# Attention before two MLPs on one core: score transposes as two 64-row halves, chained between value products and scores

## The chip, the cores and the metric

One core of a Trainium2 chip runs the whole program in one launch. The metric is the device time in microseconds (us) of that core, taken as the median of several runs. The engines are TensorE (PE; its weight loads are listed as PEld), VectorE (DVE), ScalarE (ACT), GpSimd (POOL) and the DMA queues, some of which SyncE (SP) issues.

## The reference

Attention with a causal mask and a forgetting bias, for 4 batches of 8 heads, 576 positions and 64 features per head, and then two MLPs over 2304 tokens of width 512 (hidden width 2048):

```python
scores = scale * np.matmul(q, k.transpose(0, 1, 3, 2))
cum = np.cumsum(np.maximum(s, 0.0), axis=-1)
bias = -(cum[:, :, :, None] - cum[:, :, None, :])
scores = np.where(causal, -1000000000.0, scores + np.minimum(bias, 0.0))
attn = np.exp(scores - max); attn = attn / (sum + 1e-09)
x = (attn @ v) as 2304 x 512
h = relu(x @ w_in) ** 2;  x = h @ w_out          # first MLP
h = leaky_relu(x @ w2_in, 0.01);  out = h @ w2_out   # second MLP
```

All weights of the MLPs come as 64-bit floats and are turned into 32-bit words on the chip.

## The kernel before, in words

**Attention** (`attention`, line 650) works through 16 pairs of heads. A pair takes seven steps (`STEPS`, line 77): a kind and a head `e`. Kind 0 is the first two row tiles of 128 queries, kinds 2 and 3 the third and the fourth, kind 4 the last 64 rows of both heads at once. One step is one *slot* `y` of the loop at line 775; there are 7 x 16 = 112 slots (`end`) and some more to drain. In what follows a pair's slots are counted from its own start (`k0`), so that slot 7 of a pair is slot 0 of the next.

For each kind the score products (`scores`, line 445; matmuls at lines 468 and 456) fill one PSUM bank for each head. For kinds 0, 2 and 3 each head has its own 64 rows of the array (`64*128` in the profile); kind 4 uses all 128 rows. `maxima` (line 473, DVE) masks and reduces, `exponentials` (line 504, ACT) writes the tile `t`. Two slots later (`LAG = 2`) `flip` (line 512) transposes `t` on TensorE in 128x128 pieces (line 518, and line 532 for the last 64 keys) into a PSUM bank with the tag `tr`, one head at a time, and lines 784 and 786 copy it to `pT` with DVE or ACT. `values` (line 537, matmuls at line 554) multiplies by v: the first 256 queries (region 0) in slot 5, the other 320 (region 1) in slot 9. Both heads share a bank, each with 64 columns of the array (`128*64`). `gather` (ACT, line 564) takes the result out one slot later, `inverse` and `widen` prepare the reciprocal row sums, `spread` (lines 584 and 587) transposes them, `scale` (lines 593 to 598) multiplies, and `store` (line 729) writes the pair's result to the DRAM tile `xscr` in slot 12.

**Work beside attention.** The first MLP's up product (`up1`, line 618, matmuls at line 642) goes over 5 blocks of tokens (`BLOCKS`); blocks 0 to 2 are filled in between the attention slots by `fill` (line 746), in three parts a slot. Block j may begin behind slot `START[j] = 28 * (j + 1) + 10`; blocks 0 and 1 are spread so that they end 5 slots before the next start (line 756). Their input is read from `xscr` and rounded into two parts (`up1_x`, line 606: an SP DMA in its first step, ACT line 602 and DVE line 603 in its second) at the slots `START[j]` plus the pairs of gaps in line 713, one pair for each of the four chunks of 128 features. Weight chunks are turned into words by `load_w` (slots 11 to 54) and by `convert` (19 chunks, line 740, from slot `end - 49` on). `later` holds these jobs by slot.

**The order on an engine.** The program's order is a proposal: a scheduler with a simulated timeline reorders instructions within their dependences. `in_order` (line 316) chains the instructions of an engine from a given place on; `after` (line 308) keeps what is issued inside it behind given instructions. PSUM has 4 banks for `tr`, 2 for `h`, and 2 that are one buffer `S` for scores. From pair 5 on (`x >= PLAIN`, `AHEAD = 20` score groups) one group of scores is held ahead, before that two, and the products of the first five pairs are in plain fp32 and not in split parts.

```python
tiles = ((0, 0, P), (1, P, 3 * P)) if kind == 0 else ((kind, 0, (kind + 1) * P),)
...
jobs = flip(at, zx, *STEPS[zs], live.pop(z))
for i, (out, src) in enumerate(jobs):
    if STEPS[zs][1] == 0 and (i == 0 or zx > PLAIN):
        nc.vector.tensor_copy(out, src)
    else:
        nc.scalar.activation(out, src, AF.Copy)
```

After attention come blocks 3 and 4, the first MLP's down product and the second MLP (`down`, `up`, line 839), which the change does not touch.

Of the kernel before, what the change touches and what calls it, by code (L numbers as in the profile page):

```python
# [23 lines left out]
def attention_then_two_mlps(  # L24
# [24 lines left out]
    nc = tc.nc  # L49
# [16 lines left out]
    EARLY = (1, 7, 6, 5)  # L66
    LEAD = 3
    BEFORE = 19
    TB, VB, YB = 3, 4, 2
    GB1, XS, XF = 3, 5, 3  # L70
    QK_SCALE = 1.0 / float(D) ** 0.5
    PASSES = ((0, 0), (0, 1), (1, 0))
# [26 lines left out]
    def bank(tag):  # L99
        return ps.tile([P, 512], F32, tag=tag, name=tag, bufs=dict(tr=4, h=2)[tag])  # L100
# [236 lines left out]
    def running_sums(at, ag):  # L337

        sp, cum = [at.tile([BH, S], F32, tag="t", name="t", bufs=TB) for _ in range(2)]
        one, neg = [at.tile([BH, S], F32, tag="pT0", name="one", bufs=2) for _ in range(2)]  # L340
        ka = at.tile([BH, 2, S], F32R, tag="pT1", name="ka", bufs=2)
        nc.sync.dma_start(sp, s.rearrange("b h t -> (b h) t"))
        nc.gpsimd.memset(one, 1.0)
        nc.gpsimd.memset(neg, -1.0)
        nc.vector.memset(f32(ag[:, 1]), 0.0)
        for e in range(2):
            nc.gpsimd.memset(f32(ag[64 * e:64 * e + 4, 1]), -1.0)
        nc.vector.memset(f32(ag[:, 0]), 1.0)
        yield
        nc.vector.tensor_scalar(sp, sp, 0.0, 1.0 / QK_SCALE, ALU.max, ALU.mult)  # L350
        raw["sums"] = nc.vector.tensor_tensor_scan(cum, one, sp, 0.0, ALU.mult, ALU.add).ins
        nc.vector.tensor_copy(ka[:, 0], cum)
        nc.vector.tensor_tensor(ka[:, 1], cum, f32(ka[:, 0]), ALU.subtract)
        h0, h1 = pairs[0].h
        for z in range(2):
            raw["sent"] = nc.sync.dma_start(f32(ag[z:z + 65:64, 1]), f32(ka[h0:h1 + 1:h1 - h0, z])).ins
            nc.scalar.dma_start(f32(ag[2 + z:z + 67:64, 0]), f32(ka[h0:h1 + 1:h1 - h0, z]))
        yield
        nc.gpsimd.dma_start(aug[:, 0:2, 1], f32(ka))
        stored = nc.gpsimd.dma_start(aug[:, 2:4, 0], f32(ka))  # L360
        with after(stored.ins):
            nc.gpsimd.dma_start(aug[:, 0:2, 0], one.unsqueeze(1).to_broadcast([BH, 2, S]))
            nc.gpsimd.dma_start(aug[:, 2:4, 1], neg.unsqueeze(1).to_broadcast([BH, 2, S]))
# [145 lines left out]
                                        accum_out=sums[:, s0:s0 + 1])  # L509
        return done.ins  # L510

    def flip(at, x, kind, e, t):

        p = pairs[x]
        w = 3 * P if kind == 0 else min((kind + 1) * P, 4 * P)
        tr = bank("tr")
        for c in range(w // P):
            nc.tensor.transpose(tr[:, c * P:(c + 1) * P], t[:, c * P:(c + 1) * P], ident)  # L518
        trv = tr[:, :w].rearrange("p (c i) -> p c i", i=P)
        if kind == 0:  # L520
            p.pT[0, e] = at.tile([P, 3 * P], F32, tag="pT0", name="pT0", bufs=2)
            return [(p.pT[0, e], tr[:, :w])]
        if kind < 4:
            if kind == 2:
                p.pT[1, e] = at.tile([P, 4, NR1], F32, tag="pT1", name="pT1", bufs=2)
            off = kind * P - R
            return [(p.pT[1, e][:, 0:kind + 1, off:off + P], trv)]
        jobs = []
        for h in range(2):
            jobs.append((p.pT[1, h][:, :, 2 * P:], trv[:, :, 64 - 64 * h:P - 64 * h]))  # L530
        tr = bank("tr")
        nc.tensor.transpose(tr[:, :P], t[:, S - P:], ident)
        p.pX = at.tile([P, 2, 64], F32, tag="pX", name="pX")
        jobs.append((p.pX.rearrange("p h i -> p (h i)"), tr[:, :P]))
        return jobs

    def values(x, region):

        p = pairs[x]
        po = bank("tr")  # L540
        n = R if region == 0 else NR1
        mm = []
        for c in range(2 if region == 0 else 5):
            if region == 0:
                mm.append((c, c * P, [p.pT[0, e][:, c * R:R + c * P] for e in range(2)]))
            elif c < 4:
                a = max(0, c * P - R)
                mm.append((c, a, [p.pT[1, e][:, c, a:] for e in range(2)]))
# [101 lines left out]
    def attention(at, mg, mx):  # L650
# [59 lines left out]
        for j in range(B):  # L710
            for c in range(KC):
                job = up1_x(mx, j, c, XS)
                for gap in ((-8, -6), (-7, -4), (-5, -3), (-5, -2))[c]:
                    at_slot(START[j] + gap, step, job)

        for x in range(len(pairs)):
# [23 lines left out]
        for ch in range(BEFORE):  # L740
            job = convert(*divmod(ch, FC), stage, nc.sync, 3)
            for gap in range(6):
                at_slot(end - 5 * BEFORE // 2 - 2 + 5 * ch // 2 + gap, step, job)
        units, block, done = None, -1, 0

        def fill(y, part):

            nonlocal units, block, done
            anchor = pairs[-1].anchor if y >= end + 3 else None
            if units is None and block + 2 < B and y > START[block + 1]:  # L750
                block, done = block + 1, 0
                units = up1(mg, block)
            if units is None:
                return
            a = START[block]
            stop = START[block + 1] - 5 if block + 2 < B else end + 10

            def parts(z, part):
                return (z - a) * 3 + part

            while units is not None and done * parts(stop, -2) < parts(y, part + 1) * (4 * FC + 1):
                if block == B - 2 and anchor is not None:
                    with tc.issue_after(anchor):
                        step_units()
                else:
                    step_units()
# [5 lines left out]
            done += 1  # L772

        live, anchors = {}, [None, None]
        for y in range(end + 13):
            x, st = divmod(y, n)
            z = y - LAG
            jobs = []
            if 0 <= z < end:
                zx, zs = divmod(z, n)  # L780
                jobs = flip(at, zx, *STEPS[zs], live.pop(z))
                for i, (out, src) in enumerate(jobs):
                    if STEPS[zs][1] == 0 and (i == 0 or zx > PLAIN):
                        nc.vector.tensor_copy(out, src)  # L784
                    else:
                        nc.scalar.activation(out, src, AF.Copy)
            if y < end:
                args = maxima(at, x, *STEPS[st])
                live[y] = args[0]
                behind = [args[-1], exponentials(*args[:-1])]  # L790
            fill(y, 0)
            if y + 1 < end and STEPS[(y + 1) % n][1] == 0:
                last = len(KINDS) * x + KINDS.index(STEPS[st][0])
                while asked <= last + (2 if last + 2 < AHEAD else 1):
                    scores(asked // len(KINDS), KINDS[asked % len(KINDS)])
                    asked += 1
            for px in (x - 1, x):
                if not 0 <= px < len(pairs):
                    continue
                k0 = y - n * px  # L800
                if k0 == 6:
                    gather(at, px, 0, pairs[px].po)
                if k0 == 8:
                    scale(px, 0, pairs[px].rb)
                if k0 == 10:
                    gather(at, px, 1, pairs[px].po)
                if k0 == 12:
                    scale(px, 1, pairs[px].rb)
                    store(px)
                if k0 == 5:  # L810
                    pairs[px].po = values(px, 0)
                if k0 == 9:
                    pairs[px].po = values(px, 1)
# [6 lines left out]
                if k0 == 7:  # L820
                    pairs[px].rb = spread(px, 0)
                if k0 == 11:
                    pairs[px].rb = spread(px, 1)
            fill(y, 1)
            with after(*anchors, raw["last"]):
                for f, args in later.pop(y, ()):
                    f(*args)
# [309 lines left out]
```

## Time and profile before

| | |
|---|---|
| three runs | 954.41, 958.48, 959.14 us; median 958.48 us |
| profiled execution | 960.39 us |
| its span, first to last instruction | 958.6 us |
| PE, PEld, DVE, ACT, POOL busy | 97%, 86%, 75%, 61%, 19% of the span |
| attention slots in the trace | about 10.7 to 337 us, blocks 3 and 4 until about 421 us |

In the rows, `128*128 128x384 f32` is rows times columns of the array, then what is written. Merged rows of the timeline give the start, the time to the end of the last, and the number of instructions; matmuls overlap, so their pace is read from one row's start to the next row's start, or from a row's length less the last one's own time. A number in square brackets is idle time of the engine before the row and what ended it.

### The profile page before, as it was taken

Reading aid. Unit: us, or ns where it says so; the run is one execution under the profiler, and the core shown is the slowest. Engines: PE = TensorE matmul, PEld = TensorE weight load, DVE = VectorE, ACT = ScalarE, POOL = GpSimd, SP = SyncE. Lnnn points to the kernel's source line nnn. Section 1 sums busy time; section 2 is a strip of 40 time slices with the busy share of each in tenths; the row PEclk is TensorE's granted clock in tenths of the full one; section 3 lists DMA queues with packets and bytes.
Section 4 is the critical chain, followed back from the end, with each engine's and each line's share of the span. In section 5 each row is a group of like instructions: output and inputs, shape, how many; then the busy total and the mean of one; then the engine's idle time right before and its main releaser. Section 6 shows DMA issues by size and latency. Waiting matters only on the chain.

```text
span 958.6 us, 15689 instructions
## 1 busy us (share of the span) xinstructions
PE 928.1 (97%) x5502; PEld 828.4 (86%) x5502; DVE 715.4 (75%) x1307; ACT 580.2 (61%) x1072; POOL 180.9 (19%) x301
## 2 busy tenths in 40 slices
PE   6989999999989989999999999999999999999997
PEld 4656777777767768899999999899999999999997
DVE  7799664756766537769898899688568788786974
ACT  5788766777667644437565555667567764444442
POOL 4467642223333000000112200101111000000000
PEclk9999999999989999999999999999999999999999
DMA  9866827484954547784938733756858673717303
GB/s 165 199 163 176 225 67 184 147 221 152 252 166 148 174 149 261 254 275 156 319 118 273 254 120 110 256 195 238 315 201 310 211 264 114 199 38 210 100 10 57
DMA packets 229566, 178.43 MB, mean 186 GB/s; under 512 B 139600, under 2 KB 206352, under 8 KB 229488
## 3 DMA queue, kind: packets, MB, share of 16 engines
q1 hardware_dynamic: 192568, 105.13, 40.1%
q10 hardware_dynamic: 27048, 38.16, 10.9%
q0 software_dynamic: 9872, 34.15, 10.3%
q8 instruction: 43, 0.70, 0.3%
q14 instruction: 35, 0.29, 0.1%
HBM read 111.25 MB, written 66.13 MB: 185 GB/s over the span
## 4 chain that ended last, share of the span: by engine, by line
PE 49%; issue 7%; DMA 3%; DVE 3%; ACT 1%; POOL 1%; POOLq 0%; ACTq 0%; SPq 0%; DVEq 0%
PE q L839 42%; PE h L642 7%; DMA wst<-in_moe_w_out_dram 1%; DVE op L946 1%; DMA gp<-qscr 1%; PE tr L554 0%; DMA xh<-xscr 0%; POOL zscr L1008 0%; DVE gp L938 0%; DVE gp L940 0%; DMA gscr<-gs 0%; DMA wb<-wscr 0%; POOL wscr L185 0%; DVE w L198 0%; DVE gp L942 0%
## 5 line engine op out<-in xcount | busy, mean ns | idle before, releaser
L839 PE MATMUL q<-op,w 128*128 128x384 f32 x3024 | 527.6, 335 | 5.2 <-ACT post L892 2.8
L839 PEld LDWEIGHTS q<-op,w 128*128 128x128 f32 x3024 | 523.6, 188 | 8.9 <-DVE op L946 4.2
L945 ACT ACTIVATE op<-gp 128x768 fp32r<-128x768 f32 x189 | 158.2, 846 | 151.3 <-PE q L839 133.3
L642 PE MATMUL h<-xs,w 128*128 128x512 f32 (+1 forms) x960 | 218.9, 379 | 2.9 <-ACT xs L602 2.5
L946 DVE TENSOR_TENSOR op<-gp,op 128x768 fp32r<-128x768 f32 x189 | 177.8, 952 | 40.8 <-ACT op L945 39.5
L642 PEld LDWEIGHTS h<-xs,w 128*128 128x128 f32 x960 | 164.0, 190 | 34.7 <-ACT xs L602 3.3
L508 ACT ACTIVATE t<-t,m 128x128 f32<-128x128 f32 (+2 forms) x144 | 83.4, 580 | 50.7 <-DVE m L484 48.2
L484 DVE CUSTOM_DVE_ANT_0 t<-S,mask 128x128 f32<-128x128 f32 (+2 forms) x129 | 58.0, 475 | 62.6 <-PE S L468 40.9
L185 POOL DMA_DIRECT2D wscr<-wt x48 | 26.5, 552 | 244.2 <-DVE wt L122 231.5
L625 ACT ACTIVATE gs<-h 128x512 f32<-128x512 f32 (+1 forms) x80 | 43.7, 550 | 46.3 <-PE h L642 45.8
L518 PE MATMUL tr<-ident,t 128*128 128x128 f32 x384 | 66.7, 285 | 3.2 <-ACT t L508 1.9
L518 PEld LDWEIGHTS tr<-ident,t 128*128 128x128 f32 x384 | 44.2, 142 | 24.3 <-issue 6.8
L912 DVE TENSOR_TENSOR post<-q,post 128x768 f32<-128x768 f32 (+1 forms) x55 | 51.6, 939 | 15.5 <-PE q L839 15.1
L554 PE MATMUL tr<-pT,v 128*64 128x320 f32 (+3 forms) x384 | 56.2, 400 | 3.6 <-DVE pT L784 2.7
L122 DVE SCALAR_TENSOR_TENSOR wt<-wst,wt 128x512 uint32<-128x512 uint32 x64 | 54.8, 856 | 2.1 <-POOL wt L121 1.4
L892 ACT ACTIVATE post<-q 128x768 f32<-128x768 f32 (+1 forms) x56 | 43.8, 781 | 12.6 <-PE q L839 12.5
L468 PE MATMUL S<-Y 64*128 64x128 f32 (+3 forms) x324 | 41.9, 377 | 9.3 <-DVE Y L426 7.5
L113 ACT ACTIVATE wt<-wst 128x512 f32<-128x512 f32 x64 | 42.3, 661 | 14.0 <-DMA wst<-in_moe_w_in_dram 7.9
L554 PEld LDWEIGHTS tr<-pT,v 128*64 128x64 f32 x384 | 28.6, 140 | 25.0 <-issue 5.2
L117 DVE TENSOR_SCALAR wt<-wt 128x512 uint32<-128x512 uint32 x64 | 32.3, 504 | 21.2 <-ACT wt L113 21.0
L872 ACT ACTIVATE post<-post 128x768 f32<-128x768 f32 x36 | 30.4, 846 | 24.8 <-DVE post L912 24.7
L784 DVE COPY pT<-tr 128x384 f32<-128x384 f32 (+2 forms) x74 | 38.3, 526 | 9.4 <-PE tr L518 9.2
(119 smaller groups left out, 933.5 us busy)
## 6 DMA issues: line engine op xcount, KB each, us to landing
gscr<-gs ACTq DMA_DIRECT2D x36, 512.0 KB
gp<-gscr SPq DMA_DIRECT2D x48, 384.0 KB
qscr<-post ACTq DMA_DIRECT2D x48, 384.0 KB
gp<-qscr SPq DMA_DIRECT2D x48, 384.0 KB
wscr<-wt POOLq DMA_DIRECT2D x48, 256.0 KB, 4.2
wst<-in_moe_w_in_dram SPq DMA_DIRECT2D x19, 512.0 KB
wst<-in_moe_w_out_dram SPq DMA_DIRECT2D x16, 512.0 KB
wst<-in_moe_w_out_dram POOLq DMA_DIRECT2D x16, 512.0 KB, 5.4
```

The costliest lines, as they stand in the source:

```text
L122: nc.vector.scalar_tensor_tensor(t, hw, 0xC0000000, t, ALU.bitwise_and, ALU.bitwise_or)
L484: return nc.vector.tensor_tensor_reduce(t[:, a:z], sc, msk, -QK_SCALE, first, ALU.add, ALU.min, m).ins
L508: done = nc.scalar.activation(t[:, a:z], t[:, a:z], AF.Exp, bias=m[:, c:c + 1], scale=-1.0, accum_out=sums[:, s0:s0 + 1])
L518: nc.tensor.transpose(tr[:, c * P:(c + 1) * P], t[:, c * P:(c + 1) * P], ident)
L554: p.anchor = nc.tensor.matmul(po[64 * e:64 * e + 64, a:n], p.vr[:, c, e], rhs[e], start=(y == 0), stop=(y == len(mm) - 1), skip_group_chec ...
L625: done = nc.scalar.activation(g, h[:, :w], AF.Relu)
L642: nc.tensor.matmul(h[:, :w], win[fc][:, a, c * P:(c + 1) * P], xs[j, c][:, z, :w], start=(c == 0 and y == 0), stop=(c == KC - 1 and y == 2))
L839: i = nc.tensor.matmul(*args, skip_group_check=True, **kw).ins
L892: done = nc.scalar.activation(t[:, xs], acc, AF.Copy)
L912: done = nc.vector.tensor_tensor(t[:, xs], acc, t[:, xs], ALU.add)
L945: a = nc.scalar.activation(t[:, 0], src, AF.Copy)
L946: c = nc.vector.tensor_tensor(t[:, 1], src, f32(t[:, 0]), ALU.subtract)
```

## The change

`flip` now handles both heads of a kind in one call, in the slot in which the second head's turn has come (slots 3, 5, 7 for kinds 0, 2, 3, slot 8 for kind 4). Each 128x128 piece becomes two transposes of 64 rows, which go to two `tr` banks; copies out are made per row half, kinds 3 and 4 with DVE, kinds 0 and 2 with ACT. The call moves behind the value products, which move one slot later (6 and 10), and in front of the scores; the three are chained on TensorE, and the second part of the slot's `up1` work is kept behind them. `gather`, `scale`, `spread` and `store` move one slot later. Blocks 0 and 1 of `up1` end 1 slot before the next start, the rounding of chunks 1, 2 and 3 moves to slots -1, 0 and 0 of the start (their loads to -7, -4 and -4), conversions start 6 slots sooner. `t` has 4 buffers (3 before), `v` 3 (4 before).

```diff
-    TB, VB, YB = 3, 4, 2
+    TB, VB, YB = 4, 3, 2
...
-    def flip(at, x, kind, e, t):
+    def flip(at, x, kind, ts):
         p = pairs[x]
-        w = 3 * P if kind == 0 else min((kind + 1) * P, 4 * P)
-        tr = bank("tr")
-        for c in range(w // P):
-            nc.tensor.transpose(tr[:, c * P:(c + 1) * P], t[:, c * P:(c + 1) * P], ident)
...
+        banks = [bank("tr") for _ in range(2)]
+        w = 3 if kind == 0 else kind + 1
+        n = 0
+        for t in ts:
+            for c in range(w):
+                a = min(c * P, S - P)
+                for r in range(2):
+                    hs = slice(64 * r, 64 * r + 64)
+                    nc.tensor.transpose(banks[r][:, 64 * n:64 * n + 64], t[hs, a:a + P], ident[hs, hs])
+                n += 1
...
+        for r in range(2):
+            src = banks[r][:, :64 * n].rearrange("p (e c i) -> p e c i", e=len(ts), i=64)
+            if kind == 0:
+                jobs.append((p.pT[0][:, :, :, 64 * r:64 * r + 64], src))
+            elif kind < 4:
+                off = kind * P - R + 64 * r
+                jobs.append((p.pT[1][:, :, 0:w, off:off + 64], src))
+            else:
+                jobs.append((p.pT[1][:, 1 - r, :, 2 * P:], src[:, 0, 0:4]))
+                jobs.append((p.pX[:, r], src[:, 0, 4]))
+        for out, src in jobs:
+            if kind > 2:
+                nc.vector.tensor_copy(out, src)
+            else:
+                nc.scalar.activation(out, src, AF.Copy)
...
-                for gap in ((-8, -6), (-7, -4), (-5, -3), (-5, -2))[c]:
+                for gap in ((-8, -6), (-7, -1), (-4, 0), (-4, 0))[c]:
...
-                at_slot(end - 5 * BEFORE // 2 - 2 + 5 * ch // 2 + gap, step, job)
+                at_slot(end - 5 * BEFORE // 2 - 8 + 5 * ch // 2 + gap, step, job)
...
-            stop = START[block + 1] - 5 if block + 2 < B else end + 10
+            stop = START[block + 1] - 1 if block + 2 < B else end + 10
...
             fill(y, 0)
+            tiled = len(nc.cur_bb.bb.instructions)
+            for px in (x - 1, x):
+                if not 0 <= px < len(pairs):
+                    continue
+                k0 = y - n * px
+                if k0 == 6:
+                    pairs[px].po = values(px, 0)
+                if k0 == 10:
+                    pairs[px].po = values(px, 1)
+            if 0 <= z < end:
+                zx, zs = divmod(z, n)
+                kind, e = STEPS[zs]
+                if e or kind == 4:
+                    flip(at, zx, kind, [live.pop(i) for i in range(z - e, z + 1)])
             if y + 1 < end and STEPS[(y + 1) % n][1] == 0:
                 last = len(KINDS) * x + KINDS.index(STEPS[st][0])
                 while asked <= last + (2 if last + 2 < AHEAD else 1):
                     scores(asked // len(KINDS), KINDS[asked % len(KINDS)])
                     asked += 1
+            in_order(tiled, (nc.tensor.engine,))
+            divided = [i for i in nc.cur_bb.bb.instructions[tiled:] if i.engine == nc.tensor.engine][-1:]
...
-            fill(y, 1)
+            with after(*divided):
+                fill(y, 1)
```

## Rows read from the trace of the kernel before

**Rows 1.** Windows, pairs 10, 12, 13: length, busy time and count by engine, clock, DMA.
```profile
196.80:222.10 25.30, 25.30 (x162) 19.65 (x161) 16.00 (x48) 17.82 (x42) 8.60 (x14) 1.00 0.72 188
...
246.90:267.50 20.60, 17.35 (x125) 12.70 (x123) 17.55 (x54) 14.62 (x36) 7.16 (x12) 1.00 1.02 276
267.50:294.00 26.50, 26.31 (x145) 18.78 (x146) 15.53 (x39) 18.27 (x43) 8.65 (x14) 0.87 0.42 132
```

**Rows 2.** The same windows, line 642 alone (PE, then PEld).
```profile
196.80:222.10 25.30, 15.29 (x61) 11.19 (x62) 1.00 0.72 188
...
246.90:267.50 20.60, 6.55 (x24) 4.21 (x24) 1.00 1.02 276
267.50:294.00 26.50, 13.60 (x48) 9.47 (x48) 0.87 0.42 132
```

**Rows 3.** Waits of PE between 85 and 340 us: total, times, longest.
```profile
PE h L642 <- ACT xs L602: 2.5, 1, 2.5
PE tr L518 <- ACT t L508: 1.4, 1, 1.4
PE tr L554 <- DVE pT L784: 1.3, 1, 1.3
PE S L456 <- DVE m L484: 0.8, 1, 0.8
```

**Rows 4.** Timeline of PE in pair 10: start, us, line, form, count.
```profile
196.87 4.81 PE L642 MATMUL h<-xs,w 128*128 128x512 f32 x20
...
201.55 0.48 PE L642 MATMUL h<-xs,w 128*128 128x512 f32 x1
201.96 0.78 PE L468 MATMUL S<-Y 64*128 64x384 f32 x6
202.58 0.34 PE L468 MATMUL S<-ag 64*128 64x384 f32 x2
202.85 0.44 PE L518 MATMUL tr<-ident,t 128*128 128x128 f32 x2
203.22 2.16 PE L554 MATMUL tr<-pT,v 128*64 128x320 f32 x16
205.21 0.28 PE L554 MATMUL tr<-pX,v 128*64 128x64 f32 x4
205.42 0.55 PE L518 MATMUL tr<-ident,t 128*128 128x128 f32 x3
```

**Rows 5.** Timeline of PEld, same stretch.
```profile
201.96 0.47 PEld L468 LDWEIGHTS S<-Y 64*128 64x128 f32 x6 [0.25 <-issue]
...
202.85 0.20 PEld L518 LDWEIGHTS tr<-ident,t 128*128 128x128 f32 x2 [0.25 <-issue]
```

**Rows 6.** Timeline of ACT and PE around block 2's start.
```profile
267.01 0.63 ACT L602 ACTIVATE xs<-xh 128x512 fp32r<-128x512 f32 x1 [1.72 <-DMA xh<-xscr]
...
267.69 1.22 PE L642 MATMUL h<-xs,w 128*128 128x512 f32 x2 [2.54 <-ACT xs L602]
```

**Rows 7.** The chain that ended last, near the end of attention: start, us, what.
```profile
347.31 2.36 DMA xscr<-xo
...
349.69 3.98 DMA xh<-xscr
```

**Rows 8.** Windows in which the granted clock was 0.50.
```profile
267.47:274.29 6.82, 6.60 (x19) 3.94 (x20) 6.29 (x14) 5.92 (x18) 3.18 (x3) 0.50 0.05 8
339.15:342.56 3.41, 3.32 (x13) 2.79 (x15) 0.56 (x3) 0.00 (x0) 0.28 (x1) 0.50 0.20 77
```

**Rows 9.** Groups by line and form until 460 us: count, busy us, mean ns.
```profile
L784 DVE COPY pT<-tr 128x384 f32<-128x384 f32 x32 | 17.6, 549 | 6.4 <-PE tr L518 6.4
...
L786 ACT ACTIVATE pT<-tr 128x384 f32<-128x384 f32 x32 | 15.2, 479 | 8.7 <-PE tr L518 8.2 <-ACT gs L627 0.4
...
L784 DVE COPY pT<-tr 128x512 f32<-128x512 f32 x16 | 11.0, 688 | 2.9 <-PE tr L518 2.8
```

**Rows 10.** Windows of an early pair (3).
```profile
49.40:62.30 12.90, 12.02 (x83) 8.08 (x83) 12.58 (x32) 11.12 (x32) 9.40 (x13) 1.00 0.43 120
```

More of the change, by code (lines that the diff above doesn't have):

```diff
@@ L339, in running_sums @@
         sp, cum = [at.tile([BH, S], F32, tag="t", name="t", bufs=TB) for _ in range(2)]
-        one, neg = [at.tile([BH, S], F32, tag="pT0", name="one", bufs=2) for _ in range(2)]
-        ka = at.tile([BH, 2, S], F32R, tag="pT1", name="ka", bufs=2)
+        one = at.tile([BH, S], F32, tag="pT0", name="one")
+        neg = at.tile([BH, S], F32, tag="v", name="neg", bufs=VB)
+        ka = at.tile([BH, 2, S], F32R, tag="pT1", name="ka")
         nc.sync.dma_start(sp, s.rearrange("b h t -> (b h) t"))
@@ L510, in exponentials @@
         return done.ins
-    def flip(at, x, kind, e, t):
+    def flip(at, x, kind, ts):
         p = pairs[x]
-        w = 3 * P if kind == 0 else min((kind + 1) * P, 4 * P)
-        tr = bank("tr")
-        for c in range(w // P):
-            nc.tensor.transpose(tr[:, c * P:(c + 1) * P], t[:, c * P:(c + 1) * P], ident)
-        trv = tr[:, :w].rearrange("p (c i) -> p c i", i=P)
-        if kind == 0:
[L521 to L527, printed above, removed]
-        jobs = []
[L529 to L535, printed above, removed]
+        banks = [bank("tr") for _ in range(2)]
[8 more added lines that the diff above has]
+                n += 1
+        if kind == 0:
+            p.pT[0] = at.tile([P, 2, 3, P], F32, tag="pT0", name="pT0")
+        if kind == 2:
+            p.pT[1] = at.tile([P, 2, 4, NR1], F32, tag="pT1", name="pT1")
+        if kind == 4:
+            p.pX = at.tile([P, 2, 64], F32, tag="pX", name="pX")
+        jobs = []
+        for r in range(2):
[13 more added lines that the diff above has]
+                nc.scalar.activation(out, src, AF.Copy)
@@ L544, in values @@
             if region == 0:
-                mm.append((c, c * P, [p.pT[0, e][:, c * R:R + c * P] for e in range(2)]))
+                mm.append((c, c * P, [p.pT[0][:, e].rearrange("p c i -> p (c i)")[:, c * R:R + c * P] for e in range(2)]))
             elif c < 4:
                 a = max(0, c * P - R)
-                mm.append((c, a, [p.pT[1, e][:, c, a:] for e in range(2)]))
+                mm.append((c, a, [p.pT[1][:, e, c, a:] for e in range(2)]))
             else:
@@ L774, in attention @@
         live, anchors = {}, [None, None]
-        for y in range(end + 13):
+        for y in range(end + 14):
             x, st = divmod(y, n)
             z = y - LAG
[L778 to L786, printed above, removed]
             if y < end:
@@ L800, in attention @@
                 k0 = y - n * px
-                if k0 == 6:
+                if k0 == 7:
                     gather(at, px, 0, pairs[px].po)
-                if k0 == 8:
+                if k0 == 9:
                     scale(px, 0, pairs[px].rb)
-                if k0 == 10:
+                if k0 == 11:
                     gather(at, px, 1, pairs[px].po)
-                if k0 == 12:
+                if k0 == 13:
                     scale(px, 1, pairs[px].rb)
                     store(px)
[L810 to L813, printed above, removed]
                 if k0 == 5:
@@ L819, in attention @@
                     widen(at, px, 1)
-                if k0 == 7:
+                if k0 == 8:
                     pairs[px].rb = spread(px, 0)
-                if k0 == 11:
+                if k0 == 12:
                     pairs[px].rb = spread(px, 1)
-            fill(y, 1)
+            with after(*divided):
+                fill(y, 1)
             with after(*anchors, raw["last"]):
```

## The prediction, made before the changed kernel ran

> **What bounds the kernel now.** I read the windows first, cut at the first exponential of each pair. Pair 10 is an ordinary pair with fill work: TensorE is busy for all of its 25.30 us, DVE for 16.00 and ACT for 17.82 [rows 1]. So here the order of the other engines costs nothing as long as TensorE never waits, and what counts is TensorE's own work. Of it, 61 matmuls are `up1` work [rows 2], at 0.23 us each (20 of them take 4.81 us [rows 4], less the tail of the last one: 0.23). That leaves 25.30 - 61 x 0.23 = 11.3 us of TensorE for one pair of attention. The same sum for pair 12 gives 20.60 - 24 x 0.23 = 15.1 us and for pair 13 26.50 - 48 x 0.23 = 15.5 us [rows 1, 2]: these two lose 3.8 + 4.2 = 8.0 us against an ordinary pair. The waits say where: in the whole stretch from 85 to 340 us TensorE has only four waits, 6.0 us in all, and the longest, 2.5 us, is for the rounding of x [rows 3]. Just behind that wait the granted clock is 0.50, the 1.2 GHz level, for 6.82 us [rows 8]; before it TensorE had been idle for 2.54 us [rows 6]. So there are two places to save: TensorE's work in each pair, and that hole.
>
> **Transposes.** A pair has 6 + 6 + 8 + 5 = 25 pieces of 128x128. In a row two of them take 0.44 us and three 0.55 [rows 4], so one costs 0.11 us. What sets that is the stream, not the load: the second load of a row starts 0.06 us behind the first (two loads of about 0.14 us take 0.20 together [rows 5]). The value products stream at the same pace: two matmuls for each product make 2 x (3 x 320 + 192) = 2304 columns a head, the heads side by side, from 203.22 to 205.21 [rows 4], 0.86 ns a column, and 128 columns at that pace are 0.11 us. A half streams 64 columns, 0.055 us. Two halves lie on different rows of the array and go to different banks, as the two heads' scores do: six score matmuls of 384 columns took 0.62 us up to the next row [rows 4], where one after the other, at the pace of `up1`, they would need 6 x 0.23 x 384/512 = 1.04; their six loads lie within 0.47 us too [rows 5]. So I take one piece, as two halves side by side, at 0.06 us, the time of the load: 25 x 0.06 = 1.5 us a pair in place of 25 x 0.11 = 2.75, **1.25 us less**. The bounds: 0.055 (stream alone, 1.4 us less) and 0.12 (halves one after the other, 0.25 us more).
>
> **Changes of array mode.** The halves work in the 64-row mode of the scores, where they were in the full mode of `up1`. One visit to the scores, from the last `up1` matmul at 201.55 to the transpose at 202.85 [rows 4], takes 1.30 us; the `up1` matmul is 0.23 of it and four pairs of 384 columns 0.69, so 0.38 is entering and leaving, and the uncovered load of the next transpose (0.06 [rows 5]) makes it 0.44 us. The same for the value products (203.22 to 205.42, less 2432 columns at 0.86 ns, plus about 0.1 on entering and 0.06 for the next load) gives 0.3 us. So one change of mode costs 0.15 to 0.22 us; I take 0.2. Before, a pair has ten: the groups of kinds 0, 2 and 3 and two value groups, each entered and left (kind 4 is in full mode). After: slot 0 flips alone (2), slot 1 flips and scores of kind 2 together (2), slot 3 values, flip, scores of kind 3 (3), slot 5 flip, then kind 4 in full mode (2), slot 6 values and scores (3). That is twelve, **0.4 us more** (bounds: nothing to 0.44).
>
> The Trainium skill's page "TensorEngine Tiling (Array Packing)", section "Key Properties", says that changing the tiling mode drains TensorE. The prices in the paragraph above agree. It speaks against a change that adds changes of mode: by that rule alone the sum would be 11 x 0.4 = 4.4 us longer than before, 962.9 us.
>
> Together a pair has 0.85 us less work on TensorE. In pairs 5 to 15 TensorE is the bound, and all `up1` work that is not done there is done right behind on TensorE, so the saving reaches the end: 11 x 0.85 = **9.4 us**.
>
> **Early pairs.** In pairs 0 to 4 other engines limit as well: pair 3 has DVE busy for 12.58 of 12.90 us, TensorE for 12.02 [rows 10]. The copies change there. Until pair 5 DVE did two copies of 384 columns, one of 512 and one of 256; now two of 512, two of 256, two of 64. From 0.549 and 0.688 us [rows 9] a column costs 1.1 ns above a base of 0.13, so 256 are 0.41 and 64 are 0.20: 2.20 us before, 2.60 after, 0.4 more. ACT loses a copy of 512 and gains two of 384 (0.479 each [rows 9]), less the kind 4 copies. With DVE the bound, five pairs cost 2 us more; with TensorE the bound they gain 4. I take nothing. In later pairs ACT gets some 0.4 us and DVE loses some 0.3 a pair; both have over 7 us of room in pair 10 [rows 1].
>
> **The hole.** Blocks 0 and 1 now end one slot before the next start, and chunks 2 and 3 of x have four slots from load to rounding where they had two and three. The store and the load behind it took 2.36 and 3.98 us [rows 7], 6.3 us in all, which two short slots don't hold: ACT stood 1.72 us for the load with the exponentials behind it [rows 6]. The store comes a slot later, and so does the load, so the queue on SP keeps its order (the load waits for the store's landing, and the conversions and the loads of q, k and v stand behind it, as before). Three slots without fill remain where there were seven. Chunk 1's rounding must now wait for the buffer that block j's first chunk leaves only in its last hidden chunk; that is one slot earlier, so I charge nothing. Of the 8.0 us I take 5 as saved (bounds 0 and 8.0).
>
> **The tail.** After the last maxima TensorE waits 1.4 us for an exponential and 1.3 us for a copy of `pT` [rows 3] and then has the lower clock for 3.41 us [rows 8], which costs up to half of that: 4.4 us. Conversions that start six slots sooner clear DVE's and ACT's queues there, but `store` comes a slot later and one more slot drains. I take 1 us (bounds 0 and 4.4). In the middle the same conversions only move; the engines have room for them. Buffers: `t` is held a slot longer by the first head and has one more; `v` lives from its load to slot 10, 19 slots, and three buffers cover 21. I cost both at nothing.
>
> **Sum.** 9.4 + 5 + 1 = 15.4 us less. The profiled execution took 960.39 us, so it would be 945.0; that run is 1.9 us above the median of 958.48, against which I forecast **943.1 us**.
>
> **Rivals.** (a) *The halves don't overlap*, so the edit doesn't do what it is built for: 25 x 0.12 = 3.0 us, 0.25 + 0.4 = 0.65 us more a pair, 7.2 us in all, against 6 for the hole and tail: 959.7 us. For it: no transpose in half rows is in the trace. Against it: the scores do overlap [rows 4]. (b) *The hole stays or moves* to the new, later block starts, since rounding now falls right before the first use: only the 9.4 us remain, 949.1 us. For it: the wait was on a chain store, load, rounding that is still there. (c) *The chain makes TensorE wait*: values wait for copies of `pT`, flips for exponentials, scores behind both, and the second part of the slot's fill may not pass them. There are five chains a pair, 55 in pairs 5 to 15. At 15.4 / 55 = 0.28 us a chain the gain is gone, from 0.37 us on the kernel is slower than the measurement's limit; with 0.55 us each it is 30.3 - 15.4 = 14.9 us slower, 973.4 us. Against it: with two slots (about 7 us) between exponential and flip, TensorE had a single wait of that kind in 255 us [rows 3], in the tail. For it: one wait of 0.8 us for maxima [rows 3] shows that scores are just in time where fill is short.
>
> **How the numbers follow.** A measurement of this kernel can tell about 0.5% (4.8 us) from no change. Forecast 0.60, (b) 0.15, (a) 0.11, (c) 0.14. Faster is the forecast and (b): 0.75; same is (a): 0.11; slower is (c): 0.14. The range: the lower end takes the best bounds, 1.4 x 11 + 8.0 + 4.4 = 27.8 us less, 931; the upper end takes in (b) with 2 us for the early pairs (951) and the cases between it and (a), 957. It leaves out (c) and a part of (a).
>
> **What would show it.** Right: an ordinary pair near 10.5 us beside its `up1` matmuls; pairs of half transposes every 0.06 us; twelve changes of mode a pair; no wait on line 602 and no lower clock near 267 us. Wrong: halves 0.06 us apart one by one (a); waits of TensorE for line 602 at the later starts (b); more than 0.28 us of wait for `t`, `pT` or `m` in each chain (c). The forecast fails as a whole if an ordinary pair is not shorter.

## The result, and the profile after

| | before | after |
|---|---|---|
| median of six runs | 958.75 us | 951.0 us (948.31 to 951.52) |
| ratio, 95% interval | | 0.9902 (0.9877 to 0.9927) |
| profiled execution, span | 960.39, 958.6 us | 948.31, 946.5 us |
| pair 5's first exponential at | 80.1 us | 80.2 us |
| from there to the end of block 4's `up1` | 341.0 us | 327.7 us |
| the rest of the span | 537.5 us | 538.6 us |
| changes of array mode a pair (pairs 6 to 14) | 10.9 | 14.0 |

The kernel is 7.8 us or 1.0% faster, where 15.4 us were forecast. The times by part are read from the timelines, the changes of mode are counted in them. The profiled execution happens to be the fastest of the six; another profile of the same kernel (e5, below) is more like the others. The rest of the span, behind the work that the change touches, takes 536.5 to 539.4 us in the profiles of this document; so 3 us between two profiled executions can come from there.

The windows of pairs 10, 12 and 13 of the changed kernel, as in [rows 1]:

```profile
188.40:210.50 22.10, 22.10 (x177) 16.42 (x176) 15.76 (x44) 16.39 (x40) 7.39 (x12) 1.00 0.84 225
234.20:258.80 24.60, 24.60 (x187) 17.44 (x185) 15.93 (x49) 18.31 (x43) 8.08 (x14) 1.00 0.86 220
258.80:277.90 19.10, 18.61 (x155) 13.12 (x154) 17.27 (x51) 16.64 (x41) 8.17 (x14) 1.00 0.60 182
```

The same windows for line 654 (the `up1` matmuls) alone, as in [rows 2]:

```profile
188.40:210.50 22.10, 12.99 (x51) 8.86 (x50) 1.00 0.84 225
234.20:258.80 24.60, 14.21 (x55) 9.20 (x53) 1.00 0.86 220
258.80:277.90 19.10, 8.93 (x32) 5.56 (x33) 1.00 0.60 182
```

Beside its `up1` matmuls (50, 53 and 31 that start in the pair, at 0.23 us) pair 10 has 10.6 us, where it had 11.3. Pairs 12 and 13 have 12.4 and 12.0 where they had 15.1 and 15.5: better, but over an ordinary pair by 1.8 and 1.4 us. Pairs 8 and 9, which were ordinary before (11.3 and 11.6 us by the same sum), have become longer: 11.7 and 12.2. The granted clock is 1.00 in all three windows. And TensorE's waits between 85 and 340 us, four with 6.0 us in [rows 3], have become one:

```profile
PE tr L524 <- ACT pT L547: 0.3, 1, 0.3
```

So what pairs 12 and 13 have too much is hardly waiting. The timeline of TensorE shows what an ordinary chain looks like, here in slot 3 of pair 10 (start, us, line, form, count):

```profile
197.59 2.16 PE L566 MATMUL tr<-pT,v 128*64 128x320 f32 x16
199.58 0.28 PE L566 MATMUL tr<-pX,v 128*64 128x64 f32 x4
199.79 0.59 PE L524 MATMUL tr<-ident,t 64*128 64x64 f32 x12
200.19 0.94 PE L469 MATMUL S<-Y 64*128 64x512 f32 x6
```

The weight loads of the same halves, in the timeline of PEld:

```profile
199.79 0.45 PEld L524 LDWEIGHTS tr<-ident,t 64*128 64x128 f32 x12
```

Twelve halves, six pieces, take 0.40 us up to the scores, 0.06 us a piece behind the first load; before, three whole pieces had 0.55 us in their row [rows 4]. There is no change of mode between the halves and the scores. Pair 12 looks otherwise:

```profile
253.30 0.65 PE L566 MATMUL tr<-pT,v 128*64 128x256 f32 x2
253.87 0.96 PE L654 MATMUL h<-xs,w 128*128 128x512 f32 x3
254.76 0.86 PE L566 MATMUL tr<-pT,v 128*64 128x256 f32 x6
255.56 1.65 PE L654 MATMUL h<-xs,w 128*128 128x512 f32 x6
257.14 0.34 PE L524 MATMUL tr<-ident,t 64*128 64x64 f32 x4
257.29 0.93 PE L469 MATMUL S<-Y 64*128 64x128 f32 x12
```

`up1` matmuls stand inside the group of value products and between it and the halves, though all three are chained. The chain gives an order; it does not keep other work out. Work that was proposed ahead of the chain, such as the first part of the slot's fill, may still be put between its links (e9 tests this). Pair 12 has 17 changes of mode, pair 10 has 12.

The early pairs went the other way. TensorE's waits between 10 and 85 us in the changed kernel, the five longest:

```profile
PE tr L566 <- DVE pT L545: 4.8, 4, 1.4
PE tr L524 <- ACT xo L576: 4.6, 3, 2.0
PE S L469 <- DVE m L485: 2.7, 2, 1.5
PE tr L596 <- DVE pT L545: 1.7, 2, 1.3
PE h L654 <- ACT xs L614: 1.7, 1, 1.7
```

The three longest of the kernel before in the same stretch, of 6.0 us in all:

```profile
PE S L468 <- DVE m L484: 1.9, 2, 1.2
PE tr L554 <- DVE pT L784: 1.3, 2, 1.0
PE tr L518 <- ACT pT L786: 0.7, 1, 0.7
```

Value products wait for copies of `pT`, flips for `gather` to leave a bank, scores for maxima: 16 us in place of 6. In this execution the waits take what TensorE has saved in work: between 10 and 80 us it is busy for 56.4 us where it was for 63.8, and pair 5 begins 0.1 us later. The wait of 1.7 us for `xs` is new too; it stands at the start of block 0, and it is there without the chain too (1.2 us in e6, 0.9 in e7 and e12).

### The profile page after: what moved, and what is told of

Read it like the earlier page. It is cut to its first block, busy times and chain, and to the rows that moved or that the text cites. A ratio compares the mean times of both kernels' runs of the same rounds, so it can differ in the third digit from the quotient of the medians.

```text
span 946.5 us, 16461 instructions
## 1 busy us (share of the span) xinstructions
PE 910.5 (96%) x5902; PEld 806.3 (85%) x5902; DVE 708.1 (75%) x1319; ACT 577.9 (61%) x1076; POOL 182.8 (19%) x301
## 4 chain that ended last, share of the span: by engine, by line
PE 46%; issue 9%; DVE 7%; DMA 6%; ACT 2%; POOL 1%; SPq 0%; POOLq 0%; DVEq 0%; ACTq 0%
PE q L855 33%; PE h L654 11%; DVE op L962 3%; DMA gp<-gscr 1%; DMA gp<-zscr 1%; DMA wst<-in_moe_w_out_dram 1%; DMA gp<-qscr 1%; PE tr L566 1%; DVE gp L956 1%; DVE gp L958 1%; DMA zscr<-post 1%; PE tr L524 1%; PE S L469 1%; POOL zscr L1024 1%; DVE wt L121 0%
## 5 line engine op out<-in xcount | busy, mean ns | idle before, releaser
L654 PEld LDWEIGHTS h<-xs,w 128*128 128x128 f32 x960 | 161.0, 189 | 40.2 <-issue 5.8
L509 ACT ACTIVATE t<-t,m 128x128 f32<-128x128 f32 (+2 forms) x144 | 83.3, 580 | 53.6 <-DVE m L485 48.8
L928 DVE TENSOR_TENSOR post<-q,post 128x768 f32<-128x768 f32 (+1 forms) x55 | 51.6, 940 | 15.9 <-PE q L855 15.5
L566 PE MATMUL tr<-pT,v 128*64 128x320 f32 (+3 forms) x384 | 51.8, 389 | 4.9 <-DVE pT L545 4.8
L524 PEld LDWEIGHTS tr<-ident,t 64*128 64x128 f32 x800 | 33.0, 138 | 25.6 <-issue 11.2
L122 DVE SCALAR_TENSOR_TENSOR wt<-wst,wt 128x512 uint32<-128x512 uint32 x64 | 48.6, 759 | 3.7 <-POOL wt L121 3.0
L566 PEld LDWEIGHTS tr<-pT,v 128*64 128x64 f32 x384 | 25.1, 136 | 30.7 <-issue 7.6
L524 PE MATMUL tr<-ident,t 64*128 64x64 f32 x800 | 43.1, 231 | 5.1 <-ACT xo L576 4.6
L117 DVE TENSOR_SCALAR wt<-wt 128x512 uint32<-128x512 uint32 x64 | 32.6, 510 | 16.8 <-ACT wt L113 16.7
L198 DVE TENSOR_TENSOR w<-wq,w 128x512 fp32r<-128x512 f32 x49 | 33.3, 687 | 14.3 <-ACT w L197 14.2
```

Of the source, the lines that this page charges most:

```text
L122: nc.vector.scalar_tensor_tensor(t, hw, 0xC0000000, t, ALU.bitwise_and, ALU.bitwise_or)
L509: done = nc.scalar.activation(t[:, a:z], t[:, a:z], AF.Exp, bias=m[:, c:c + 1], scale=-1.0, accum_out=sums[:, s0:s0 + 1])
L524: nc.tensor.transpose(banks[r][:, 64 * n:64 * n + 64], t[hs, a:a + P], ident[hs, hs])
L654: nc.tensor.matmul(h[:, :w], win[fc][:, a, c * P:(c + 1) * P], xs[j, c][:, z, :w], start=(c == 0 and y == 0), stop=(c == KC - 1 and y == 2))
L928: done = nc.vector.tensor_tensor(t[:, xs], acc, t[:, xs], ALU.add)
```

## The experiments

Each has its own runs of the kernel before on the same chip (958.93 us for e1 to e4, 959.98 for e5 to e8, 959.29 for e9 to e12); ratios are against these. "Late part" is the stretch from pair 5's first exponential to the end of block 4's `up1`, the fifth row of the table above. The first four take the change apart.

**e1, the schedule alone**

```diff
 # kernel before
-    for gap in ((-8, -6), (-7, -4), (-5, -3), (-5, -2))[c]:
+    for gap in ((-8, -6), (-7, -1), (-4, 0), (-4, 0))[c]:
-    at_slot(end - 5 * BEFORE // 2 - 2 + 5 * ch // 2 + gap, step, job)
+    at_slot(end - 5 * BEFORE // 2 - 8 + 5 * ch // 2 + gap, step, job)
-    stop = START[block + 1] - 5 if block + 2 < B else end + 10
+    stop = START[block + 1] - 1 if block + 2 < B else end + 10
```

> The kernel before with three edits of the change alone: blocks end one slot before the next start, rounding of x at -1, 0, 0, conversions six slots sooner. Theory S (split gain: the halves save about 0.75 us in each of 11 pairs, the later blocks and roundings close the hole near 267 us): 953 to 955 us, no wait on the rounding of x over 1 us near 267 us. Rival H (the halves are everything): 957 to 960 us. Rival P (the schedule is everything): 949 to 952 us.

Measured: 959.75 us, ratio 1.0009 (0.9993 to 1.0024). The hole near 267 us is closed as expected, and it brings nothing; the time is the one that rival H named. TensorE's longest waits between 85 and 355 us, and the one for the rounding of x:

```profile
PE h L642 <- ACT gs L625: 2.0, 1, 2.0
PE tr L518 <- ACT t L508: 1.8, 2, 1.0
...
PE h L642 <- ACT xs L602: 0.2, 1, 0.2
```

The window of the lower clock that follows the longest of them, which ends at 351.7 us:

```profile
352.51:355.92 3.41, 3.41 (x9) 2.41 (x8) 2.07 (x4) 2.60 (x6) 0.00 (x0) 0.51 0.98 336
```

The wait for the rounding fell from 2.5 to 0.2 us, but a wait of 2.0 us for `up1`'s own output came in behind attention, with a stretch of the lower clock. The late part is 1.6 us shorter than before, but pair 5 begins 1.2 us later, within 6.8 us of the lower clock (from 76.0 us), where the kernel before had 3.4 us.

**e2, the halves alone**

```diff
 # changed kernel
-    for gap in ((-8, -6), (-7, -1), (-4, 0), (-4, 0))[c]:
+    for gap in ((-8, -6), (-7, -4), (-4, -2), (-4, -1))[c]:
-    at_slot(end - 5 * BEFORE // 2 - 8 + 5 * ch // 2 + gap, step, job)
+    at_slot(end - 5 * BEFORE // 2 - 2 + 5 * ch // 2 + gap, step, job)
-    stop = START[block + 1] - 1 if block + 2 < B else end + 10
+    stop = START[block + 1] - 5 if block + 2 < B else end + 10
```

> The changed kernel with the schedule of before: blocks end five slots before the next start, rounding two, two and three slots behind the loads as before (loads of chunks 2 and 3 at -4, as the later store demands), conversions at their old slots. Theory S: 953 to 956 us, an ordinary pair still at 10.6 us of TensorE beside its fill, a wait for the rounding of x back at block 2. Rival H: 950 to 952. Rival P: 957 to 960.

Measured: 956.98 us, 0.9981 (0.996 to 1.0002), 2 us less than before and a little outside each theory's numbers. It has 15.8 changes of mode a pair and four waits of 0.5 to 1.1 us at 180 to 182 and 272 to 274 us, the last with 3.4 us of the lower clock behind it; a wait for the rounding of x did not come back. The late part is 335.4 us, 5.6 less than before, but pair 5 begins 2.8 us later. So the two parts of the change do not add: +0.8 and -2.0 us alone, -7.8 together. The halves bring more with the new schedule; which of its edits they need is not shown.

**e3, whole pieces in the same chain**

```diff
 # changed kernel
-        for t in ts:
-            for c in range(w):
-                a = min(c * P, S - P)
-                for r in range(2):
-                    hs = slice(64 * r, 64 * r + 64)
-                    nc.tensor.transpose(banks[r][:, 64 * n:64 * n + 64], t[hs, a:a + P], ident[hs, hs])
-                n += 1
+        for e, t in enumerate(ts):
+            for c in range(w):
+                a, tr, z = (min(c * P, S - P), banks[e], c) if c < 4 else (S - P, banks[1], 0)
+                nc.tensor.transpose(tr[:, z * P:(z + 1) * P], t[:, a:a + P], ident)
```

The copies keep their engines and read the other layout.

> The changed kernel, but each piece is transposed whole (128 rows, full mode), both heads in one call, chained as before, same copies by engine. Theory S: 25 pieces at 0.11 instead of 0.06 us, 1.25 us more a pair, less three changes of mode at 0.2 us (nine a pair instead of twelve): 0.65 us more in each of 11 to 16 pairs, 7 to 10 us above the changed kernel, 958 to 961 us. Rival M (only the calmer chain and the schedule matter, the stream of the transposes is hidden): 949 to 952 us.

Measured: 962.06 us, 1.0036 (1.0015 to 1.0058), 11 us above the changed kernel. Theory S holds in kind, the time is 1 us above its numbers; rival M falls. Six pieces, then the scores:

```profile
207.39 0.88 PE L521 MATMUL tr<-ident,t 128*128 128x128 f32 x6
208.20 0.97 PE L469 MATMUL S<-Y 64*128 64x512 f32 x6
```

0.81 us where the halves have 0.40. There are 12.4 changes of mode a pair, so the halves win although they add 1.6. Not all of the 11 us is transposes: TensorE waits 4.6 us in the late part, where the changed kernel waits 2.5 to 2.9.

**e4, upper halves first, then lower halves**

```diff
 # changed kernel
-        for t in ts:
-            for c in range(w):
-                a = min(c * P, S - P)
-                for r in range(2):
+        n = len(ts) * w
+        for r in range(2):
+            hs = slice(64 * r, 64 * r + 64)
+            for z in range(n):
+                a = min(z % w * P, S - P)
+                nc.tensor.transpose(banks[r][:, 64 * z:64 * z + 64], ts[z // w][hs, a:a + P], ident[hs, hs])
```

> The changed kernel with all upper halves first and then all lower halves, so that neighbours lie on the same rows of the array. Theory S (halves overlap only when neighbours lie on different rows): pieces cost 0.12 instead of 0.06 us, 1.5 us more a pair, 17 to 24 us above the changed kernel, 967 to 975 us. Rival O (halves are cheap by themselves, overlap or not): within 3 us of the changed kernel, 948 to 954 us.

Measured: 961.21 us, 1.003 (1.0007 to 1.0052): 10 us above the changed kernel. Rival O falls; theory S is right in kind, but the price is about half of what it says. The timeline of slot 3 says why:

```profile
205.44 0.58 PE L523 MATMUL tr<-ident,t 64*128 64x64 f32 x9
205.83 0.47 PE L469 MATMUL S<-Y 64*128 64x512 f32 x1
205.86 0.34 PE L523 MATMUL tr<-ident,t 64*128 64x64 f32 x3
206.01 0.94 PE L469 MATMUL S<-Y 64*128 64x512 f32 x5
```

The program has six upper halves, six lower halves, then the scores; the records show a score matmul's start ahead of the last three halves. In the single records the twelve starts form two series of six, most of them 0.06 us apart; the second begins 0.18 us behind the first. So the lower halves began while upper ones were still to come: twelve took some 0.55 us, not 0.72.

**e5, the changed kernel once more**

> The changed kernel as it is, once more on this chip, for its time beside the next three and for a second profile. Its first profile was of its fastest execution (948.31 us, mean clock 0.998), the others had 0.993 to 0.995. Theory C (its other executions lose time to the lower clock, at places where TensorE is idle early on): 950 to 952 us, and a profile with at least one more stretch of the lower clock before 90 us. Rival: the difference between executions lies in DMA, with no such stretch.

Measured: 951.38 us, 0.9917 (0.9894 to 0.9941); the profiled execution took 951.36 us. Theory C holds. The two windows of the lower clock (0.50, the 1.2 GHz level):

```profile
51.95:58.78 6.83, 5.13 (x26) 2.47 (x22) 4.02 (x15) 2.93 (x7) 4.82 (x6) 0.50 0.40 130
86.09:92.91 6.82, 6.04 (x34) 3.30 (x36) 6.82 (x16) 5.29 (x14) 5.98 (x7) 0.50 0.04 15
```

The timeline of TensorE in the second of them, with the wait that ended there:

```profile
86.87 1.22 PE L654 MATMUL h<-xs,w 128*128 128x512 f32 x2 [1.26 <-ACT xs L614]
```

In all that is 13.65 us of the lower clock up to the end of `up1`, where the kernel before had 3.4 us at 76.3 us and the two windows of [rows 8], 13.64 us in all. In this execution the change has moved the lower clock, not removed it: from the starts of the late work to the early pairs and to block 0's start, where the first `up1` matmuls now wait for x (in the kernel before TensorE has no such wait there). In the faster execution profiled above, only 3.4 us of the lower clock are left, at 51.2 us. Here pair 5 begins at 83.3 us (3.2 later than before), the late part is 329.7 us (11.3 less), the rest 536.5: together 9.0 less, 949.6 in place of 958.6 us.

The next two ask what the chain does, and e8 moves one flip. In e6, e7 and e12 the chain goes together with the hold on the second part of the fill, so the two are not told apart.

**e6, no chain before pair 5**

```diff
 # changed kernel
-            in_order(tiled, (nc.tensor.engine,))
+            if y >= n * PLAIN:
+                in_order(tiled, (nc.tensor.engine,))
-            with after(*divided):
+            with after(*(divided if y >= n * PLAIN else ())):
```

> The changed kernel with the chain and the fill behind it only from pair 5 on. Theory E (the chain makes TensorE wait in the early pairs, 13.5 us idle there against 6.0 before): idle time of TensorE before pair 5 falls to 7 to 9 us and the median by 3 to 5 us, to 946 to 948. Rival: the early waits come from copies for both heads on one engine and from two banks a flip, not from the order; 950 to 952 us.

Measured: 951.29 us, 0.993 (0.9903 to 0.9958). The waits are right in kind, the time is not: TensorE's waits between 10 and 90 us fall from 18.9 us (e5) to 11.9, less far than theory E said, and pair 5 begins at 79.7 us, 3.6 sooner. But the late part takes 331.7 us, 2.0 more, and the median stays, at the number of the rival. The 11.9 us that are left are twice the 6.0 of the kernel before. The slower transposes of e3 and e4, with the chain in place, have 10.6 and 9.4 us of waits between 10 and 85 us, where the changed kernel has 16.3. So the early waits are the chain's only in part. That TensorE also waits because it is done sooner fits with this, but is not shown further.

**e7, no chain at all**

```diff
 # changed kernel
-            in_order(tiled, (nc.tensor.engine,))
-            with after(*divided):
-                fill(y, 1)
+            fill(y, 1)
```

> The changed kernel without the chain on TensorE and without holding fill behind it, in all pairs. Theory E: it gains early (3 to 5 us) and loses late, since the scheduler then puts full-mode work between value products, flips and scores: over 15 changes of mode a pair where the changed kernel has 13.8, so 950 to 953 us in all. Rival (the chain buys nothing late): 946 to 948 us, as in the run with the chain from pair 5 on.

Measured: 961.22 us, 1.0019 (0.9999 to 1.0039), far above either number. The late part takes 343.2 us, more than the kernel before. Two visits to the value products where one would do, each followed by `up1`:

```profile
194.68 0.65 PE L566 MATMUL tr<-pT,v 128*64 128x256 f32 x4
195.26 0.96 PE L654 MATMUL h<-xs,w 128*128 128x512 f32 x3
196.15 0.44 PE L566 MATMUL tr<-pT,v 128*64 128x128 f32 x4
196.52 1.66 PE L654 MATMUL h<-xs,w 128*128 128x512 f32 x6
```

There are 16.7 changes of mode a pair. They are not all of it: TensorE also waits 2.5 us for `m` at 122 us, and the late part has 13.7 us of the lower clock, 6.8 of them around that wait, where e5 has 6.8 in all. Without the chain and the hold the halves give nothing.

**e8, kind 3's flip one slot sooner**

```diff
 # changed kernel
-            if 0 <= z < end:
-                zx, zs = divmod(z, n)
-                kind, e = STEPS[zs]
-                if e or kind == 4:
-                    flip(at, zx, kind, [live.pop(i) for i in range(z - e, z + 1)])
+            for z in (y - LAG, y - 1):
+                if 0 <= z < end:
+                    zx, zs = divmod(z, n)
+                    kind, e = STEPS[zs]
+                    soon = kind == 3 and zx >= PLAIN
+                    if (e or kind == 4) and z == y - (1 if soon else LAG):
+                        flip(at, zx, kind, [live.pop(i) for i in range(z - e, z + 1)])
```

> The changed kernel with kind 3's flip one slot sooner from pair 5 on (slot 6, behind the value products and in front of kind 0's scores), so that slot 0's own visit to the 64-row mode goes. Theory M (each change of mode costs about 0.2 us and the scheduler leaves a small rest of that flip as a visit by itself): two changes less in each of 11 pairs, 11.5 to 12 a pair, 4 to 5 us less, 946 to 947 us. Rival W (an exponential only one slot old makes the chain wait): 951 us or more, with waits of TensorE for t after 85 us.

Measured: 954.36 us, 0.9933 (0.9908 to 0.9958): a miss, 3 us above e5. The changes of mode did not fall (14.7 a pair): `up1` matmuls slipped between the value products and the flip. In pair 10:

```profile
215.40 0.87 PE L566 MATMUL tr<-pT,v 128*64 128x256 f32 x8
216.20 1.42 PE L654 MATMUL h<-xs,w 128*128 128x512 f32 x5
217.55 0.27 PE L524 MATMUL tr<-ident,t 64*128 64x64 f32 x1
```

No wait for `t` showed after 85 us. So the time is rival W's, but its cause is not there.

The last four chain the first part of the fill as well.

**e9, the first part of the fill in the chain**

```diff
 # changed kernel
+            opened = len(nc.cur_bb.bb.instructions)
             fill(y, 0)
...
-            in_order(tiled, (nc.tensor.engine,))
+            in_order(opened if y >= n * PLAIN else tiled, (nc.tensor.engine,))
```

> The changed kernel with the chain on TensorE from pair 5 on taking in the first part of the slot's fill too, so that nothing in full mode can slip between value products, flip and scores. Theory M (a change of mode costs about 0.2 us; the changed kernel has 13.8 a pair because up1 matmuls slip in): 12 to 12.5 a pair, 3 to 4 us less than the changed kernel, 947 to 949 us. Rival W (where nothing slips in, TensorE waits instead): the changes fall but waits of TensorE after 90 us take over 2 us more, 951 us or above.

Measured: 949.39 us, 0.988 (0.9847 to 0.9913), 2 us below e5; the intervals of the two overlap, so by the times alone this could be nothing, and it is 0.4 us above theory M's numbers. The profile says more: the late part is 324.8 us, 4.9 less than in e5 and 2.9 less than in the first profile of the changed kernel, and no wait of TensorE is left between 90 and 340 us, so rival W falls. There are 13.1 changes a pair, not quite the 12 to 12.5, and pairs 8, 9, 12 and 13 now have 10.8 to 11.0 us each beside their `up1` matmuls. The values stay together:

```profile
195.69 1.18 PE L654 MATMUL h<-xs,w 128*128 128x512 f32 x4
196.80 0.79 PE L469 MATMUL S<-Y 64*128 64x384 f32 x6
...
209.85 1.64 PE L654 MATMUL h<-xs,w 128*128 128x512 f32 x6
211.43 0.87 PE L566 MATMUL tr<-pT,v 128*64 128x256 f32 x8
212.23 0.65 PE L524 MATMUL tr<-ident,t 64*128 64x64 f32 x14
212.69 0.94 PE L469 MATMUL S<-Y 64*128 64x128 f32 x12
...
215.37 0.28 PE L524 MATMUL tr<-ident,t 64*128 64x64 f32 x2
```

The last line, two halves of kind 3's flip, is a visit that the twelve include. What is over twelve lies elsewhere. The first two lines show it in pair 10, where `up1` matmuls stand between kind 4's flip (ten halves from 195.24 us on) and kind 2's scores; in pair 11 six more stand between values and flip (234.6 us). So some work in full mode still gets between the links; from where is not shown.

**e10, both** (e9 with e8's edit)

> As e9_strict, and kind 3's flip one slot sooner from pair 5 on, so that it shares the visit of kind 0's scores. Theory M: about 10 changes a pair, 4 us less than e9_strict, 943 to 946 us. Rival W: an exponential one slot old makes the chain wait, no fewer than e9_strict's time, 948 us or above.

Measured: 948.03 us, 0.9874 (0.9839 to 0.9908), late part 324.3 us against 324.8 in e9. Below e9 by less than the intervals can tell, with as many changes (13.1 a pair). Theory M's number did not come; rival W's did, at its edge, but no wait for `t` shows in the late part.

**e11, flip in front of the value products** (e9 with the two blocks exchanged)

> As e9_strict, with the flip in front of the value products, so that slot 3 goes from full mode to 64 rows, to 64 columns, to 64 rows, to full mode: one change more a pair. Theory M: 2 to 4 us more than e9_strict. Rival (the price is for leaving and entering full mode alone, a change between the two narrow modes is free): within 1 us of e9_strict.

Measured: 953.48 us, 0.9931 (0.9898 to 0.9964), 4 us above e9, as theory M has it, though the intervals overlap. There are 15.1 changes a pair, 2.0 more than in e9, and the late part of the profile is longer by 4.0 us: over 11 pairs 4.0 / 22 = 0.18 us for one change. That is an estimate from one profile of each. TensorE's waits in the late part are 2.7 us in both, but e9 has 3.4 us of the lower clock there and e11 none; if that cost up to half of it, 1.7 us, one change would cost 0.26 us.

**e12, e9 without a chain before pair 5**

> As e9_strict, without chain or held fill before pair 5. If the time that the free early order saves until pair 5 (3.6 us in e6_chain_late against e5_after_again) reaches the end, 3 us less than e9_strict. If it is lost again at the start of block 0, which waits for the store and load of x, within 1 us of e9_strict, as the medians of e5 and e6 say.

Measured: 946.05 us, 0.9856 (0.9827 to 0.9885), 3.3 us below e9, the best of all and faster than both kernels; its interval touches the changed kernel's (0.9877 to 0.9927) at the edge. TensorE's longest early waits (10 to 90 us), 11.8 us in all:

```profile
PE tr L596 <- DVE pT L545: 2.6, 3, 1.1
PE h L457 <- DVE m L485: 2.5, 5, 0.6
PE S L469 <- DVE m L485: 2.4, 3, 1.5
```

Pair 5 begins at 78.6 us, 5.6 sooner than in e9. Here the early gain reaches the end in part; in e6 it did not. In both the late part is 2.0 us longer than with the early chain (326.8 us here). With intervals this wide the two don't contradict each other, and how much of the early gain reaches the end stays open.

## Why the prediction was right, and where it was off

It was right in the direction, the time lies in the range (931 to 957), and the size was half of the forecast: 7.8 us in place of 15.4. That 951 is also the number that the prediction has for rival (b) with 2 us lost in the early pairs is luck: the hole of pairs 12 and 13 did close for the most part, and a part of the gain went to the changes of mode. By its steps:

- **Transposes, 0.06 us a piece: right.** 0.06 us in the timeline. e3 shows that the stream was worth shortening (11 us, some of it waits), e4 that the overlap of the halves is what shortens it (10 us). Rival (a) is out: the halves overlap.
- **Changes of mode: the price was about right, the number was not.** 0.2 us was taken for one, e11 gives 0.18 to 0.26. But "twelve" took each chain for one undisturbed visit. The kernel before has 10.9 and the changed one 14.0, so 3.1 are added a pair and not 2: 1.1 x 0.2 x 11 = 2.4 us of the missing gain. The step that failed is the reading of `in_order` as "together" where it says "in this order". e9 closed a part of that, and its late part is 16.2 us shorter than that of the kernel before, as much as was forecast for the whole; its pair 5 begins 4.1 us later.
- **Ordinary pairs: nearly.** 0.7 us less in pair 10, 0.85 forecast. Pairs 8 and 9 became longer, with 15 and 18 changes of mode where they had 10 and 12.
- **Early pairs, "I take nothing": wrong in the usual execution.** Pair 5 begins 3.2 us later in e5, 0.1 in the fastest. A good part of the reason is rival (c), the chain that makes TensorE wait, which was priced for pairs 5 to 15 alone and dismissed there. Late it does not wait (0.3 us in 255); early, with slots of 1.2 to 2.4 us on average and DVE nearly full [rows 10], it does: 16 us of waits for 6, and e6 and e12 without the early chain begin pair 5 3.6 and 5.6 us sooner than e5 and e9. Whether the reason weighed there, 0.4 us more of copies on DVE, has a share in the waits that are left without the chain (11.9 us) no run tests.
- **The hole, 5 us: closed, but not as a term of its own.** The wait of 2.5 us and the lower clock behind it are gone, and of the 8.0 us of pairs 12 and 13 only 1.8 + 1.4 = 3.2 are left, so 4.8 are saved. e1 shows that the edits that close it are worth nothing alone: another wait of 2.0 us follows, and pair 5 begins later. In e5 the lower clock, counted as saved with the hole, is there again at other places, as long as before: rival (b), at block 0's start.
- **The tail, 1 us:** both waits there [rows 3] and the lower clock behind them are gone. No run takes the tail alone.

For e5 the shortfall comes out about so: 3.2 us are lost early, and 4.1 us are missing in the late part (11.3 saved of 15.4). To these the added changes of mode give 2.4 us, and the 6.8 us of the lower clock at 86 us up to half of their length, 3.4. These are estimates from one profile.

What stays open: why the halves under the old schedule (e2) have 15.8 changes a pair. That later, thinner fill leaves the scheduler fewer matmuls to slip in is only argued.

## What to carry to other kernels

A chain gives order, not closeness: where a visit to another array mode is to be paid once, the work proposed ahead of it has to be in the chain too, and the timeline has to be counted for visits before and after. Price a new order separately in the stretch where the engine is the bound and in the stretch where others are; a chain that cost next to no waiting in slots of 2.7 us and more made TensorE wait in slots of 1.2 to 2.4 us. And a gain read from a hole is only safe when the next wait behind it has been looked for: here two parts that were worth nothing and 2 us alone were worth 8 together.

## What the runs showed of the hardware that was not expected

TensorE took up halves on the lower rows, and even a score matmul, while halves ahead of them in the program's order were still to start (e4, a score's start at 205.83 us and the last three halves from 205.86): six and six took some 0.55 us, where one after the other would be 0.72. And executions of one kernel differ together with where the clock falls: up to the end of `up1` the changed kernel had 3.4 us of the lower clock in one execution (948.31 us) and 13.7 us in another (951.36 us), with 0.3 us of waits in pairs 6 to 14 of the first and none in the second. That the clock is the whole of the 3 us is not shown.
